# Four banks, an earlier cast and later gathers in the experts of a routed MoE kernel on one core

## Chip, core and metric

The kernel runs on one core of a Trainium2 chip. The metric is the device time of one execution in microseconds.

## What is computed

A linear attention with decay over 4 x 8 heads and 768 steps gives 3072 rows of 384 numbers. They go through a dense mixture block (a * b, then two products, width 1024), and then through eight experts, of which each row is sent to two: the expert's product with w1 (384 x 1024), the positive part, the product with w2 (1024 x 384), weighted and summed into the row. The work around the change is this last part; the shapes below are those of the experts' block.

```python
def _moe2_ref(x, w_gate, w_noise, noise, w1, w2) -> np.ndarray:
    N, D, E, F = (3072, 384, 8, 1024)
...
    for e in range(E):
        for k in range(2):
            mask = top2[:, k] == e
...
            h = np.maximum(x[mask] @ w1[e], 0.0)
            out[mask] += top2_w[mask, k, None] * (h @ w2[e])
    return out.astype(np.float32)

def reference(**kwargs):
...
    attn_out = _attn_ref(**attn_kwargs)
    B, H, S, D = attn_out.shape
    x = np.ascontiguousarray(attn_out.transpose(0, 2, 1, 3)).reshape(B * S, H * D)
    x = _moe_ref(x=x, **moe_kwargs)
    return _moe2_ref(x=x, **moe2_kwargs)
```

## The kernel before

**Numbers in halves.** Every factor is kept as a high part (suffix h) and a low part (suffix l), and a product is three matmuls (mm3, lines 182 to 184: high by high, high by low, low by high). The high part is made by a cast on ScalarE (ACT), the low part by a subtraction on VectorE (DVE).

**The experts.** Expert by expert, 7 row tiles are computed, in two halves: half 0 has the columns of four row tiles (512), half 1 the rest. mm1(hf, ff) is one matmul group of the first layer: nine matmuls into one PSUM bank, for one of eight blocks ff of the hidden width. ACT reads the bank (L889, HH high), then DVE (L890, HH low); then the bank is free. For half 0 the banks are those in MB (two, bA and bB, line 878), taken in turn; for half 1 there are three. mm2(e, j) is the second layer of row tile j: 24 matmuls, then ACT's weighted eviction (L907, ye) and POOL's indirect DMA that adds the rows into the output (L917). The last, small tile has its own form (L912, L914, L916).

**What expert e + 1 needs.** need(e + 1, hf, r): SP loads an index list (L809, ti), POOL gathers the rows (L857, xg). turn(e + 1, hf): SP stores the gathered rows into a buffer in memory (L863) and reads them back transposed (L869, XTx). load_e loads raw weights on SP (L790); split_e casts them (ACT L797, DVE L800). tr(e + 1, hf) casts the transposed rows (XTh: ACT L874, XTl: DVE L875). In second_half (line 931) the row tiles run in the order 0, 6, 1, 2, 3, 4, 5; a quarter of the next weights is cast behind each of the first four, tr(e + 1, 0) stands behind row tile 3 and tr(e + 1, 1) behind row tile 5. first_half(e) issues need and the weight loads for e + 1 and calls turn(e + 1, 0) and turn(e + 1, 1) behind its groups 3 and 6.

**Expert 0** is written out, since its rows come while the router still works: index_first (L817), gather_first (L826), store_first (L831), turn_first (L838); its mm1 groups of half 0 already use four banks, bA, bB, PB[4] and PB[5]. Its first four row tiles of mm2 follow, with need(1, 0, 0) behind the first of them (line 1058), then its second half; behind that turn(1, 0) and the loads of expert 1's first weights, then the remaining row tiles with split_e(1, 0, i).

**What sets the order.** DVE and POOL take their instructions in the order in which the program is written; so do SP's DMAs and those casts of ACT that are pinned with keep_in_program_order. The rest of ACT and PE is ordered by the scheduler. The first weight quarters of expert 0 are cast in the last group of the dense block, in the slots i = 0, 4, 7 and 9 (line 1014).

Of the kernel before, what the change touches and what calls it, by code (L numbers as in the profile page):

```python
# [71 lines left out]
def tile_kernel(ctx: ExitStack, tc: tile.TileContext, dt, nat, w3t, wout, w1, w2, e1, e2, cf, ci, out):  # L72
# [17 lines left out]
    def f(ap):  # L90
        return ap.bitcast(F32)
# [24 lines left out]
    PB = [psum.tile([P, 512], F32, name=f"pb{i}") for i in range(8)]  # L116
    bA, bB, bX, bY, bST, bK = PB[0], PB[1], (PB[2], PB[3]), PB[4], (PB[5], PB[6]), PB[7]
# [674 lines left out]
    def split_e(e, m, i):  # L792
        s = slice(768 * i, 768 * i + 768)
        o = 768 * (i % 2)
        src = RW[e, m, i // 2][:, o:o + 768]
        h, l = (WAh, WBh)[m][:, s], (WAl, WBl)[m][:, s]
        cast = act.copy(out=h, in_=src)  # L797
        if e or m:
            tc.keep_in_program_order(cast)
        dve.tensor_tensor(out=l, in0=src, in1=f(h), op=OP.subtract)  # L800

    def load_idx(e, hf, r):
        TI[e, hf] = EP["a"].tile([P, (TA, TB + 1)[hf], 2], I32, name=f"ti{hf}", bufs=3)
        for o, n, w, j in (((0, TA, TPT, 0),), ((HOLD, TB, TPT, 0), (CAP - TPL, 1, TPL, TB)))[hf]:
            if isinstance(r, int):
                v = table[e * CAPT + r * CAP + o:e * CAPT + r * CAP + o + w * n]
            else:
                v = table[bass.ds(r * CAP + (e * CAPT + o), w * n)]
            tc.keep_in_program_order(sp.dma_start(out=TI[e, hf][:w, j:j + n].rearrange("p j t -> p (j t)"),  # L809
                                                  in_=v.rearrange("(p j) t -> p (j t)", p=w)))  # L810
# [18 lines left out]
    def store_first(j):  # L829
        w = rows_of(j)  # L830
        tc.keep_in_program_order(sp.dma_start(  # L831
            out=rows[0, 2 * TPT * j:2 * TPT * j + 2 * w].rearrange("(p t) d -> p (t d)", t=2), in_=XG[0, j][:w]))

    def turn_first(j, m):

        hf, o = (0, 0) if m <= TPT * TA else (1, 2 * TPT * TA)
        s = slice(2 * TPT * j, 2 * m)
        tc.keep_in_program_order(sp.dma_start_transpose(  # L838
            out=XT["x", hf].bitcast(U16)[:, :, s.start - o:s.stop - o], in_=rows[0, s]))
# [15 lines left out]
    def gather(e, j, rows=NROW):  # L855
        XG[e, j] = EP["b" if e else "a"].tile([P, 2 * DM], U16, name="xg", bufs=NXG)
        pool.indirect_dma_start(out=XG[e, j][:rows_of(j)], out_offset=None, in_=x2d[:rows],  # L857
                                in_offset=bass.IndirectOffsetOnAxis(ap=ti(e, j)[:, 0:1], axis=0))
# [12 lines left out]
    def tr(e, hf):  # L871
        for db in range(3):
            x, h = XT["x", hf][:, db], XT["h", hf][:, db]
            tc.keep_in_program_order(act.copy(out=h, in_=x))  # L874
            dve.tensor_tensor(out=XT["l", hf][:, db], in0=x, in1=f(h), op=OP.subtract)  # L875

    first = True
    MB, MC, AD = (bA, bB), [1], [-1]
    NXG = 7

    def mm1(hf, ff, banks=None):
        n = NAB[hf]
        banks = banks or ((bA, bK, bB) if hf else MB)
        bank = banks[ff % len(banks)][:, :n]
        for kb in range(3):
            w = slice(kb * FF + ff * P, kb * FF + ff * P + P)
            mm3(bank, WAh[:, w], WAl[:, w], XT["h", hf][:, kb], XT["l", hf][:, kb], kb == 0, kb == 2)
        n = (TA, TB)[hf] * TPT
        act.activation(out=Hh[hf][:, ff], in_=bank[:, :n], func=AF.Relu)  # L889
        dve.scalar_tensor_tensor(Hl[hf][:, ff], bank[:, :n], 0.0, f(Hh[hf][:, ff]), op0=OP.max, op1=OP.subtract)  # L890
        if hf == 1:
            dve.tensor_scalar(HM[hf][:, ff], bank[:, n:], 0.0, None, op0=OP.max)

    def mm2(e, j, mid=None):
        hf, jj = divmod(j, TA)
        n, s = rows_of(j), slice(TPT * jj, TPT * jj + rows_of(j))
        MC[0] ^= 1
        bank = bX[MC[0]][:, :DM]
        y = EP["b"].tile([P, DM], F32, name="ye", bufs=9)
        wt = ti(e, j)[:, 1:2].bitcast(F32)  # L900
        if j < NT - 1:
            for ff in range(8):
                if mid and ff == 4:
                    mid()
                w = slice(ff * DM, ff * DM + DM)
                mm3(bank[:n], Hh[hf][:, ff, s], Hl[hf][:, ff, s], WBh[:, w], WBl[:, w], ff == 0, ff == 7)
            act.activation(out=y[:n], in_=bank[:n], func=AF.Copy, scale=wt)  # L907
        else:

            for ff in range(8):  # L910
                g = ff % 4
                pe.matmul(bank[n * g:n * g + n], HM[hf][:, ff], RW[e, 1, ff // 4][:, g * DM:g * DM + DM],  # L912
                          start=ff < 4, stop=ff > 3, tile_position=(0, n * g))
            act.activation(out=y[:n], in_=bank[:n], func=AF.Copy, scale=wt)  # L914
            for g in range(1, 4):
                dve.scalar_tensor_tensor(y[:n], bank[n * g:n * g + n], wt, y[:n], op0=OP.mult, op1=OP.add)  # L916
        ins = pool.indirect_dma_start(out=out, out_offset=bass.IndirectOffsetOnAxis(ap=ti(e, j)[:, 0:1], axis=0),  # L917
                                      in_=y[:n], in_offset=None, compute_op=OP.add).ins

        if j == 0 or AD[0] != e:  # L920
            AD[:] = [e]
        for p in AD[1:]:
            tc.declare_no_dep(ins, p, reason="an expert's rows differ")
        AD.append(ins)

    def need(e, hf, r, rows=NROW):
        load_idx(e, hf, r)
        for j in range(TA) if hf == 0 else range(TA, NT):
            gather(e, j, rows)

    def second_half(e, r, early=True):

        nx = e + 1 < E
        for ff in range(8):
            mm1(1, ff)
            if ff % 2 and early:
                split_e(e, 1, 2 + ff // 4) if ff in (1, 5) else None
        for j in (0, NT - 1, *range(1, NT - 1)):
            mm2(e, j)
            if nx and j < 4:  # L940
                split_e(e + 1, 0, j)
            if nx and j in (3, 5):
                tr(e + 1, j // 5)
        if nx:
            for i in range(2):
                load_e(e + 1, 1, i)
# [37 lines left out]
    for g in range(NGRP):  # L984
        sub = [(mo_ab, g, 0, 0), (mo_ab, g, 0, 1), None, (mo_ab, g, 1, 0), (mo_ab, g, 1, 1), (mo_x, g, 0),
               (mo_ab, g, 2, 0), (mo_ab, g, 2, 1), (mo_x, g, 1), (mo_ab, g, 3, 0), (mo_ab, g, 3, 1), (mo_x, g, 2)]
        if g == 0:
            sub[:5] = [(mo_ab, g, 0, 0, bST[0]), (mo_ab, g, 1, 0, bST[1]), None, (mo_ab, g, 0, 1, bA), (mo_ab, g, 1, 1)]
        if g == NGRP - 1:
            cvx.close()  # L990
            attx.close()
            open_a()
            load_e(0, 0, 0)
            load_e(0, 0, 1)
        for i in range(12):
            if g == NGRP - 1 and i == 7:
                store_first(TA - 1)
                turn_first(TA - 1, TPT * TA)
            if sub[i]:
                act.on = g == 0 and i < 9  # L1000
                fn, *a = sub[i]
                fn(*a)
            elif g:
                mo_x(g - 1, 3)
                mo_lz(g - 1)
                mo_out(g - 1)
            k = SPG * g + i
            run_todo(k - .5, k)
            if i % 3 != 1:
                low_p()  # L1010
            run_todo(k, k + .5)
            act.on = False
            if g == NGRP - 1:
                if i in (0, 4, 7, 9):
                    split_e(0, 0, (0, 4, 7, 9).index(i))
                    if i == 9:
                        load_e(0, 1, 0)
                        load_e(0, 1, 1)
                if i == 0:
                    turn_first(0, TPT * (TA - 1))  # L1020
                if i == 1:
                    index_first(TA - 1, 1)
                    gather_first(TA - 1, NCH - GB)
                if i == 5:
                    tr_first(0, TA - 1)
# [29 lines left out]
    for j in range(TA):  # L1055
        mm2(0, j)
        if j == 0:
            need(1, 0, 0)
            for jj in (NT - 2, NT - 1):
                store_first(jj)  # L1060
            turn_first(NT - 2, CAP)
        if j == TA - 2:
            tr(0, 1)
    need(1, 1, 0)
# [145 lines left out]
```

## Time and profile before

| | us |
|---|---|
| median of 3 runs | 892.7 (891.82 to 895.07) |
| the profiled execution | 900.07 |
| its span in the profile | 898.2 |
| PE busy | 871.3 |
| DVE, ACT, POOL busy | 496.7, 434.3, 243.4 |

Times in the rows are microseconds from the start of the span; the experts' stage begins at about 480 and ends with the span. A row of a timeline tells the start, the duration, the engine, the line of the kernel, the operation, the tile written and the tiles read, and in brackets the idle time of the engine just before it and what ended it. SPq is SP's DMA issue. "PE pb L182 <- DVE HH L890" among the waits is PE's time spent waiting for that step of DVE. Where a row carries "x3", three like instructions are taken together.

### The profile page before, as it was taken

What the parts mean: (1) busy time and instruction counts of PE and PEld (TensorE: products, weight loads), DVE (VectorE), ACT (ScalarE), POOL (GpSimd) and SP (SyncE); (2) the same over time, 40 slices, a digit from 0 to 9 for tenths busy, and PEclk for the clock granted to TensorE, in tenths of its full rate; (3) what the DMA queues carried; (4) which work ended last, traced back from release to release, by engine and by line L of the source; (5) the groups of instructions that cost most, each with busy time, mean ns of one, the idle gap of its engine ahead of it and who ended that gap; (6) DMA issues with size and microseconds to landing.
All of it is one profiled execution on the core that took longest, in us unless ns stands there. A gap on an engine that the chain in (4) does not pass through costs nothing. (4 is left out here: it accounts for less than half of the span.)

```text
span 898.2 us, 18274 instructions
## 1 busy us (share of the span) xinstructions
PE 871.3 (97%) x7333; PEld 807.0 (90%) x7333; DVE 496.7 (55%) x1215; ACT 434.3 (48%) x876; POOL 243.4 (27%) x216
## 2 busy tenths in 40 slices
PE   8999999999999999999999999999999999999994
PEld 5789899999999999999989889898898989999894
DVE  6899866857666667665472553343435335353420
ACT  5777576555556647644452443334334333433420
POOL 2000020141231231232234535216060341603122
PEclk9999999999999999999999999999999999999998
DMA  9955398474575654525145987739185582934113
GB/s 351 391 203 189 95 136 265 117 201 157 133 219 146 190 133 126 147 51 166 36 116 120 266 232 194 187 85 226 50 240 121 145 206 65 228 80 109 18 22 38
DMA packets 123583, 139.22 MB, mean 155 GB/s; under 512 B 74592, under 2 KB 103264, under 8 KB 123488
## 3 DMA queue, kind: packets, MB, share of 16 engines
q1 hardware_dynamic: 99952, 109.58, 42.8%
q0 software_dynamic: 12160, 19.72, 11.4%
q10 hardware_dynamic: 11376, 8.65, 3.0%
q8 instruction: 59, 0.97, 0.5%
q14 instruction: 36, 0.29, 0.1%
HBM read 88.12 MB, written 36.04 MB: 138 GB/s over the span
## 5 line engine op out<-in xcount | busy, mean ns | idle before, releaser
L917 POOL DMA_INDIRECT out<-ye,ti x49 | 77.5, 1582 | 232.5 <-ACT ye L907 212.0
L182 PE MATMUL pb<-XTh,WAh 128*128 128x512 f32 (+1 forms) x384 | 132.5, 346 | 4.8 <-DVE HH L890 3.9
L184 PE MATMUL pb<-XTh,WAl 128*128 128x512 f32 (+1 forms) x384 | 131.3, 342 | 0.0
L183 PE MATMUL pb<-XTl,WAh 128*128 128x512 f32 (+1 forms) x384 | 131.1, 342 | 0.1
L182 PE MATMUL pb<-WBh,HH 128*128 128x384 f32 x384 | 129.3, 337 | 0.0
L184 PE MATMUL pb<-WBh,HH 128*128 128x384 f32 x384 | 128.4, 334 | 0.0
L183 PE MATMUL pb<-WBl,HH 128*128 128x384 f32 x384 | 128.3, 334 | 0.0
L890 DVE SCALAR_TENSOR_TENSOR HH<-pb,HH 128x256 fp32r<-128x256 f32 (+1 forms) x128 | 71.2, 557 | 78.9 <-ACT HH L889 73.2
L889 ACT ACTIVATE HH<-pb 128x256 fp32r<-128x256 f32 (+1 forms) x128 | 62.5, 491 | 106.3 <-PE pb L184 101.5
L907 ACT ACTIVATE ye<-pb,ti 128x384 f32<-128x384 f32 x42 | 24.4, 582 | 139.9 <-PE pb L184 96.0
L733 POOL DMA_INDIRECT slots<-g_sc,g_si x48 | 51.3, 1068 | 134.8 <-DVE g_si L732 69.1
L182 PEld LDWEIGHTS pb<-XTh,WAh 128*128 128x128 f32 x384 | 72.0, 188 | 15.6 <-DVE HH L890 6.5
L182 PE MATMUL pb<-xh,WAh 128*128 128x256 f32 x288 | 81.6, 284 | 0.9 <-ACT WAh L797 0.9
L183 PE MATMUL pb<-xl,WAh 128*128 128x256 f32 x288 | 80.9, 281 | 0.8 <-DVE xl L339 0.8
L183 PE MATMUL pb<-xl,WBh 128*128 128x256 f32 x288 | 81.0, 281 | 0.0
L182 PE MATMUL pb<-xh,WBh 128*128 128x256 f32 x288 | 81.0, 281 | 0.0
L184 PE MATMUL pb<-xh,WBl 128*128 128x256 f32 x288 | 81.0, 281 | 0.0
L184 PE MATMUL pb<-xh,WAl 128*128 128x256 f32 x288 | 80.8, 281 | 0.0
L183 PEld LDWEIGHTS pb<-XTl,WAh 128*128 128x128 f32 x384 | 72.3, 188 | 7.8 <-DVE XTl L875 0.3
L184 PEld LDWEIGHTS pb<-XTh,WAl 128*128 128x128 f32 x384 | 72.2, 188 | 7.7 <-DVE WAl L800 0.2
L182 PEld LDWEIGHTS pb<-WBh,HH 128*128 128x128 f32 x384 | 72.1, 188 | 5.0 <-ACT WAh L797 3.8
L800 DVE TENSOR_TENSOR WAl<-raww,WAh 128x768 fp32r<-128x768 f32 x28 | 26.7, 957 | 87.8 <-ACT WAh L797 70.4
(194 smaller groups left out, 2061.4 us busy)
## 6 DMA issues: line engine op xcount, KB each, us to landing
dtc<-dt SPq DMA_DIRECT2D x24, 772.0 KB
raw<-e SPq DMA_DIRECT2D x18, 768.0 KB
raww<-e SPq DMA_DIRECT2D x14, 768.0 KB
nrk<-nat SPq DMA_DIRECT2D x24, 384.0 KB
expert_rows<-xg SPq DMA_DIRECT2D x45, 192.0 KB
rawf<-w3t SPq DMA_DIRECT2D x16, 512.0 KB
nv<-nat SPq DMA_DIRECT2D x24, 256.0 KB
out<-zeros SPq DMA_DIRECT2D x9, 576.0 KB
```

Of the source, the lines that this page charges most:

```text
L182: pin(pe.matmul(o, wh, xh, start=start, stop=False))
L183: pe.matmul(o, wh, xl, start=False, stop=False)
L184: pe.matmul(o, wl, xh, start=False, stop=stop)
L733: ins = pool.indirect_dma_start(out=table, out_offset=bass.IndirectOffsetOnAxis(ap=si[:, i, k:k + 1], axis=0), in_=SC[:, i, k, :], in_offs ...
L800: dve.tensor_tensor(out=l, in0=src, in1=f(h), op=OP.subtract)
L889: act.activation(out=Hh[hf][:, ff], in_=bank[:, :n], func=AF.Relu)
L890: dve.scalar_tensor_tensor(Hl[hf][:, ff], bank[:, :n], 0.0, f(Hh[hf][:, ff]), op0=OP.max, op1=OP.subtract)
L907: act.activation(out=y[:n], in_=bank[:n], func=AF.Copy, scale=wt)
L917: ins = pool.indirect_dma_start(out=out, out_offset=bass.IndirectOffsetOnAxis(ap=ti(e, j)[:, 0:1], axis=0), in_=y[:n], in_offset=None, com ...
```

## The change

There are four edits. (1) The first layer's half 0 of the experts 1 to 7 uses four banks in place of two. (2) tr(e + 1, 1) stands behind row tile 4 instead of row tile 5. (3) The first quarter of expert 0's w1 is cast in slot 1 of the last group instead of slot 0. (4) need(1, 0, 0), an index load and four gathers, stands behind mm2(0, 1) instead of mm2(0, 0).

```diff
--- before.py
+++ after.py
@@ -875,7 +875,7 @@
             dve.tensor_tensor(out=XT["l", hf][:, db], in0=x, in1=f(h), op=OP.subtract)
 
     first = True
-    MB, MC, AD = (bA, bB), [1], [-1]
+    MB, MC, AD = (bA, PB[4], bB, PB[5]), [1], [-1]
     NXG = 7
 
     def mm1(hf, ff, banks=None):
@@ -939,8 +939,8 @@
             mm2(e, j)
             if nx and j < 4:
                 split_e(e + 1, 0, j)
-            if nx and j in (3, 5):
-                tr(e + 1, j // 5)
+            if nx and j in (3, 4):
+                tr(e + 1, j - 3)
         if nx:
             for i in range(2):
                 load_e(e + 1, 1, i)
@@ -1011,8 +1011,8 @@
             run_todo(k, k + .5)
             act.on = False
             if g == NGRP - 1:
-                if i in (0, 4, 7, 9):
-                    split_e(0, 0, (0, 4, 7, 9).index(i))
+                if i in (1, 4, 7, 9):
+                    split_e(0, 0, (1, 4, 7, 9).index(i))
                     if i == 9:
                         load_e(0, 1, 0)
                         load_e(0, 1, 1)
@@ -1055,10 +1055,11 @@
     for j in range(TA):
         mm2(0, j)
         if j == 0:
-            need(1, 0, 0)
             for jj in (NT - 2, NT - 1):
                 store_first(jj)
             turn_first(NT - 2, CAP)
+        if j == 1:
+            need(1, 0, 0)
         if j == TA - 2:
             tr(0, 1)
     need(1, 1, 0)
```

On ACT, at the boundary between expert 1 and expert 2 (pb_72 to pb_79 are the eight banks; XTh_5968 is the second half of the rows, HH_5971 the first half of the hidden values, ti_6644 the index list of expert 1's second half):

```order
 L907 ACTIVATE ye<-pb_74,ti_6644 128x384
+L874 CAST XTh_5968<-XTx_6509 128x288 x3
 L907 ACTIVATE ye<-pb_75,ti_6644 128x384
-L874 CAST XTh_5968<-XTx_6509 128x288 x3
-L889 ACTIVATE HH_5971<-pb_72 128x512
-L889 ACTIVATE HH_5971<-pb_73 128x512
+L889 ACTIVATE HH_5971<-pb_72 128x512
+L889 ACTIVATE HH_5971<-pb_76 128x512
 L797 CAST WBh<-raw_7274 128x768
```

The three casts moved ahead of the last eviction, and the second group's bank is another one.

On POOL, at expert 0's first row tiles (tf and ti are index lists of expert 0 and expert 1; the four first L857 gather expert 1's half 0, the last three its half 1):

```order
 L826 DMA xg<-x_rows,tf 128x768
 L826 DMA xg<-x_rows,tf 32x768
-L857 DMA xg<-x_rows,ti_6544 128x768 x4
 L917 DMA out<-ye,tf 3968x384
+L857 DMA xg<-x_rows,ti_6574 128x768 x3
+L917 DMA out<-ye,tf 3968x384
+L857 DMA xg<-x_rows,ti_6574 128x768
 L857 DMA xg<-x_rows,ti_6644 128x768 x2
 L857 DMA xg<-x_rows,ti_6644 32x768
```

The gathers of half 0 moved behind the scatter of row tile 0, and the fourth of them behind that of row tile 1.

On SP, at the same place:

```order
 L817 DMA tf<-slots 128x2
 L817 DMA tf<-slots 32x2
-L809 DMA ti_6544<-slots 128x8
-L1107 TENSOR_LOAD rounds
-L1107 ISA x2
+L1108 TENSOR_LOAD rounds
+L1108 ISA x2
 L831 DMA expert_rows<-xg 128x768
 L831 DMA expert_rows<-xg 32x768
 L838 DMA_TRANSPOSE XTx_6509<-expert_rows 128x3x320
+L809 DMA ti_6574<-slots 128x8
 L809 DMA ti_6644<-slots 128x4
```

The index load of expert 1's half 0 moved behind two stores and the transpose of expert 0's last columns. Behind these rows SP's order is the same in both: four stores L863, the transpose L869, two loads L790.

## Rows read from the trace of the kernel before

**Rows 1.** First part of the page: busy time of each engine, share, instructions.

```profile
PE 871.3 (97%) x7333; PEld 807.0 (90%) x7333; DVE 496.7 (55%) x1215; ACT 434.3 (48%) x876; POOL 243.4 (27%) x216
```

**Rows 2.** Waits of PE from 480 to 898 us: total, times, longest.

```profile
PE pb L182 <- DVE HH L890: 3.9, 5, 1.8
```

**Rows 3.** Timeline of PE at the boundaries 1 to 2 and 6 to 7.

```profile
569.58 0.39 PE L184 MATMUL pb<-XTh,WAl 128*128 128x512 f32 x1
570.58 0.50 PE L182 MATMUL pb<-XTh,WAh 128*128 128x512 f32 x1 [0.61 <-DVE HH L890]
570.92 0.39 PE L183 MATMUL pb<-XTl,WAh 128*128 128x512 f32 x1
...
837.30 0.39 PE L184 MATMUL pb<-XTh,WAl 128*128 128x512 f32 x1
837.53 0.39 PE L182 MATMUL pb<-XTh,WAh 128*128 128x512 f32 x1
```

**Rows 4.** Timeline of ACT, then DVE, at the boundary 1 to 2.

```profile
567.67 0.58 ACT L907 ACTIVATE ye<-pb,ti 128x384 f32<-128x384 f32 x1 [3.89 <-remote]
568.15 1.09 ACT L874 CAST XTh<-XTx 128x288 fp32r<-128x288 f32 x3
...
568.61 1.19 DVE L875 TENSOR_TENSOR XTl<-XTx,XTh 128x288 fp32r<-128x288 f32 x3 [6.94 <-ACT XTh L874]
569.83 1.50 DVE L890 SCALAR_TENSOR_TENSOR HH<-pb,HH 128x512 fp32r<-128x512 f32 x2
```

**Rows 5.** Timeline of PE in the last group of the dense block.

```profile
435.00 0.39 PE L182 MATMUL pb<-xh,WAh 128*128 128x256 f32 x1 [0.88 <-ACT WAh L797]
```

**Rows 6.** Timelines of SP, then POOL, then PE, 476 to 500 us.

```profile
476.46 0.81 SPq L817 DMA_DIRECT2D tf<-slots  x2
...
482.26 1.04 SPq L831 DMA_DIRECT2D expert_rows<-xg  x2
485.31 1.27 SPq L838 DMA_TRANSPOSE XTx<-expert_rows  x1
486.62 1.04 SPq L809 DMA_DIRECT2D ti<-slots  x2
487.77 3.46 SPq L863 DMA_DIRECT2D expert_rows<-xg  x4
495.08 3.34 SPq L869 DMA_TRANSPOSE XTx<-expert_rows  x1
498.48 1.10 SPq L790 DMA_DIRECT2D raww<-e  x2
...
479.20 0.98 POOL L826 DMA_INDIRECT xg<-x_rows,tf  x1 [6.35 <-DMA tf<-slots]
...
481.68 0.96 POOL L857 DMA_INDIRECT xg<-x_rows,ti  x1 [0.30 <-issue]
...
485.45 0.95 POOL L857 DMA_INDIRECT xg<-x_rows,ti  x1 [0.30 <-issue]
486.70 1.64 POOL L917 DMA_INDIRECT out<-ye,tf  x1 [0.30 <-issue]
493.10 0.99 POOL L857 DMA_INDIRECT xg<-x_rows,ti  x1 [4.76 <-DMA ti<-slots]
...
491.69 0.40 PE L182 MATMUL pb<-XTh,WAh 128*128 128x288 f32 x1 [0.36 <-ACT XTh L874]
```

**Rows 7.** DMA view, 498.5 to 507 us: queue (packets, MB, share), then an issue.

```profile
q1 hardware_dynamic: 1814, 2.03, 79.5%
...
raww<-e SPq DMA_DIRECT2D x2, 768.0 KB
```

**Rows 8.** Timeline of ACT, then DVE, at expert 1's start.

```profile
507.54 0.82 ACT L797 CAST WAh<-raww 128x768 fp32r<-128x768 f32 x1
...
512.09 1.88 DVE L875 TENSOR_TENSOR XTl<-XTx,XTh 128x512 fp32r<-128x512 f32 x3
```

**Rows 9.** Windows: length; PE, PEld, DVE, ACT, POOL busy; PEclk, DMA share, GB/s.

```profile
886.00:891.20 5.20, 0.04 (x1) 0.00 (x0) 0.00 (x0) 0.58 (x1) 1.56 (x1) 1.00 0.47 65
```

## The prediction

> **What bounds the kernel now.** The page's first part comes first: TensorE (PE) is busy 871.3 of 898.2 us, DVE half of it, ACT and POOL less [rows 1]. So only two things can move the time: a wait of PE that goes or comes. The list of PE's waits over the experts' stage (480 to 898 us) is short; nearly all of it are 3.9 us in five waits for DVE's step L890 [rows 2]. The timeline of PE shows where the first of the five lies, at the boundary between expert 1 and expert 2, at 570.58, and what the same place looks like without it, between experts 6 and 7, where PE goes on at 837.53 [rows 3]. The timelines of ACT and DVE around the first boundary tell the reason [rows 4]. ACT's last eviction of expert 1 (L907) starts at 567.67; behind it in ACT's order stand the three XTh casts of expert 2's second half (568.15); DVE, which runs in program order, takes the XTl steps of these casts at 568.61 and only then, at 569.83, the HH steps (L890) of expert 2's first matmul groups. These groups have two banks in turn, so PE's third group waits until the first bank is read out. Last I read the timelines of SP and POOL where the fourth edit acts (476 to 500 us) and the rows of expert 1's start.
>
> **Four banks and the earlier cast (edits 1 and 2).** They take away the same five waits. In rows 3 the matmul after the wait starts 1.00 us behind its predecessor, where the undisturbed pair has 0.23; and the next starts 0.34 behind it instead of 0.23. A wait listed at 0.61 thus costs 0.77 + 0.11 = 0.88, that is 0.27 more than listed. Five of them: 3.9 + 5 x 0.27 = **5.2 us**. Are all five gone? A group has nine matmuls, 9 x 0.23 = 2.1 us. With four banks the fifth group is the first that needs a bank again, two groups or 4.1 us later than the third; the longest of the five waits is 1.8 [rows 2]. Edit 2 also puts the XTh casts ahead of the last L907, so that the 1.2 us of XTl and the 1.1 us of XTh [rows 4] lie beside PE's last row tile. What is late next is that L907 itself, 1.1 us behind its old place, which only releases a scatter. Either edit would do; both together give 5.2 once, not twice. The bounds are 5.2 and, if ACT's new order only moves the wait, 3.9 - 1.8 = 2.1 (the longest one stays).
>
> The Trainium skill, "TensorE: Matmul & The Clock Gate", section "HAM oscillation — how this bites in real kernels", tells of a kernel in which "Adding PSUM double-buffering gave no further gain". By that the 5.2 would be about 0; the rule fits a PE that waits for DMA, while here the wait ends with DVE's reading of a bank [rows 3], so I go by the row. It would decide in the last rival's favour.
>
> **The weight cast one slot later (edit 3).** On DVE, pp (L589) now stands ahead of WAl (L800); on ACT the cast L797 stays ahead of the eviction L586 there. PE's only wait there is 0.88 at 435.00, and it ends with ACT [rows 5]. ACT's order at this place is the same, so 0; the bounds are 0 and -0.9. The x_rows store and two evictions of ACT behind it change places by under 1 us, with 40 us until the rows are gathered.
>
> **The four gathers later (edit 4).** What goes: the gathers no longer compete with the transposes of expert 0's last columns. PE waits 0.36 for their cast at 491.69 [rows 6]. Nothing says how much of the transpose's time (485.31 to some 491) is contention; the gain is between 0 and 1.0 (the wait, and the slow start behind it), I take 0.5.
>
> What comes: four gathers (L857), their index load (L809), and with them all that SP issues behind. Step by step, all from rows 6:
> 1. The index load stood right behind that of 476.46 in SP's order. Now it stands behind the transpose L838 (485.31 + 1.27), so at 486.6. The two index loads that stood at this very place released POOL at 493.10, after 4.76 us of waiting; the index load of 476.46 released it at 479.20, 2.7 us. So the first gather starts between 489.3 and 493.1 (before: 481.68). The queue carries the transposes then, but the four gathers are gone from it: I take 491.0.
> 2. The fourth starts three pitches of 1.26 later (481.68, then 485.45 for the fourth) and a scatter (1.64 + 0.3; that of row tile 1 now stands between): + 5.7, 496.7. Before: 485.45.
> 3. Gather to the store of its rows: 3.1 at the short end (479.20 to 482.26), 5.4 at the long (485.45 to the end of the four stores' row, 487.77 + 3.46 = 491.2 less one store of 0.3). With few transfers about I take 3.2: 499.9.
> 4. Last store to transpose: 2.5 (the second of the two stores of 482.26, at 482.8, to 485.31) to 4.2 (490.9 to 495.08). I take 4.1, since L869 is the larger transpose: at 504.0 instead of 495.08, **8.9 later** (5.5 by all short ends: 489.3 + 5.7 + 3.1 + 2.5 = 500.6; 13.3 by all long ones: 493.1 + 5.7 + 5.4 + 4.2 = 508.4).
> 5. The loads of expert 1's first weights (L790, 498.48) are issued behind it and move as far. SP's queue moved 2.03 MB in 8.5 us, 239 GB/s [rows 7], so 3.3 us for one of these two 768 KB loads (0.79 MB each): the first lands at 501.8 at the earliest. If the other 0.46 MB of that stretch (stores, the transpose's rest) go ahead of it, it lands (0.46 + 0.79) / 0.239 = 5.2 us after its issue, at 503.7; this I take. It is used at 507.54 by ACT's cast, which waited for nothing then [rows 8]: a slack of 3.8 us (up to 5.7).
> 6. Behind that cast nothing has slack: DVE's XTl steps at 512.09 run without idle time before them, and PE's first group of expert 1, which goes on behind expert 0's last row tile without a gap, needs them [rows 8]. So PE waits 8.9 - 3.8 = **5.1 us** at expert 1's start; from 0 (5.5 - 5.7) to 9.5 (13.3 - 3.8).
>
> The second transfers of expert 1 (turn of its second half, w2 loads) move as well, but are used two groups and more into the expert; by expert 2 SP has caught up.
>
> The Trainium skill, "DMA: Bandwidth & Descriptors", section "Anatomy of one DMA — SWDGE (gpsimd) path", fits a transfer by 2.0 us + bytes / 436 GB/s, an estimate of 3.8 us for 768 KB; the slack would be 5.2, the loss 3.7 and the sum -2.0. The queue's rows show 239 GB/s here, so I keep 3.8 of slack.
>
> **Sum.** -5.2 - 0.5 + 5.1 = -0.6. The profiled execution took 900.07 us (span 898.2), 7.4 above the median of the runs shown; it would come to 899.5. All terms are waits of the experts' stage, so they carry over: 892.7 - 0.6 = **892.1 us**.
>
> **Rivals.**
> - Forecast: the loss at expert 1's start lies between 2.2 and 8: 889.2 to 895.0. Chance 0.64.
> - The delay is hidden: the index load lands in 2.7 us, the gathers' rows are stored at once, and the weights arrive in time (loss 0, at most 1.2). For it: the short ends exist in rows 6. Against: three steps must all be short. 892.7 - 5.7 = 887.0 to 888.2. Chance 0.18.
> - Slower by the late transpose: the gathers queue behind scatters and their landing takes the long end, expert 1 starts up to 9.5 us late, and the wait of 0.36 stays too: 892.7 - 5.2 + 9.5 = 897.0. It decides from a loss of 5.2 on. At its long end PE stands still long enough that the clock matters: in the tail PE did almost nothing from 886.00 to 891.20 and the granted clock was still 1.00 [rows 9]; a stall twice as long has no row here. For it: the two index loads at this place did take the long end. Against: what they competed with is moved away. 895.0 to 897.0, and above if the clock falls: chance 0.11.
> - The edits don't do what they say: the four banks and the cast only move the wait from the third group to a later one. Against: the fifth group comes 4.1 us later. 892.7 - 0.5 + 5.1 = 897.3. Chance 0.07.
>
> **Numbers.** 0.5% of the time, 4.5 us, is about what a measurement of this kernel can tell from no change: faster means below 888.2, slower above 897.2. Faster holds the hidden case and little of the forecast's edge: 0.18. Slower holds half of the last rival and the end of the third: 0.09. The rest, 0.73, is no change: a gain and a loss of the same size. The range, 888.0 to 896.4, leaves out most of the hidden case below and the ends of the last two above.
>
> **What the profile will show.** Right: no wait of PE for L890 at the five boundaries; the gathers L857 of expert 1's first half at about 491; L869 at about 504; a wait of some 5 us of PE at expert 1's first group, ended by ACT's cast of WAh or by DVE; pitches of 52.6 us or so between all experts behind it. Wrong: waits at L890 that remain; an L869 below 501, from which the weights would be in time; a wait that spreads to expert 1's second half because the second turn or the w2 loads come late, which I price at nothing.

## The result: slower, by a wait twice as long as forecast

The changed kernel takes 900.54 us (median of 17 runs) beside 894.47 us for the kernel before (17 runs). The ratio is 1.0064, 95% interval [1.0042, 1.0086]: 0.64% slower. On the 892.7 us that were shown ahead, this is 892.7 x 1.0064 = 898.4 us, above the forecast of 892.1 and above the upper end of the range, 896.4.

Where it went is seen on PE. Its waits from 425 us to the end in the changed kernel, in the columns of [rows 2]:

```profile
PE pb L182 <- ACT XTh L874: 7.6, 1, 7.6
PE pb L183 <- DVE XTl L875: 1.9, 1, 1.9
PE pb L680 <- DVE g_mb L663: 0.6, 1, 0.6
PE pb L182 <- issue: 0.2, 1, 0.2
```

The five waits for L890 are gone, and one long wait has come. To size both, here are the first matmuls of expert 0, 1, 2 and 7 on PE's timeline. Before (512.48 is the last matmul ahead of expert 1):

```profile
457.80 0.39 PE L182 MATMUL pb<-XTh,WAh 128*128 128x512 f32 x1
...
512.48 0.33 PE L184 MATMUL pb<-WBh,HH 128*128 128x384 f32 x1
512.65 0.40 PE L182 MATMUL pb<-XTh,WAh 128*128 128x512 f32 x1
...
565.69 0.39 PE L182 MATMUL pb<-XTh,WAh 128*128 128x512 f32 x1
...
833.41 0.39 PE L182 MATMUL pb<-XTh,WAh 128*128 128x512 f32 x1
```

After:

```profile
456.17 0.39 PE L182 MATMUL pb<-XTh,WAh 128*128 128x512 f32 x1
...
508.85 0.34 PE L184 MATMUL pb<-WBh,HH 128*128 128x384 f32 x1
516.74 0.79 PE L182 MATMUL pb<-XTh,WAh 128*128 128x512 f32 x1 [7.56 <-ACT XTh L874]
519.43 0.79 PE L183 MATMUL pb<-XTl,WAh 128*128 128x512 f32 x1 [1.89 <-DVE XTl L875]
...
573.21 0.39 PE L182 MATMUL pb<-XTh,WAh 128*128 128x512 f32 x1
...
835.57 0.39 PE L182 MATMUL pb<-XTh,WAh 128*128 128x512 f32 x1
```

Four stretches follow from them:

| stretch | before | after | difference |
|---|---|---|---|
| expert 0, first to last matmul | 54.68 | 52.68 | -2.0 |
| from that last matmul to expert 2 | 53.21 | 64.36 | +11.15 |
| expert 2 to expert 7 | 267.72 | 262.36 | -5.4 |
| up to the first matmul of expert 0 | 457.80 | 456.17 | -1.6 |

The last row lies almost wholly ahead of the change and differs from execution to execution. The profiled execution of before was a long one for its kernel (900.07 beside a median of 894.47), so the two executions are only 2.0 us apart; the medians are 6 apart. What the change itself does is the first three rows: -2.0 + 11.15 - 5.4 = +3.8 us in this pair of traces. The other 2 us of the medians have no row here; they would fit a typical execution of before that has less for the edits to win than this long one, which is not shown.

The long wait is a chain on SP, POOL and ACT, whose rows answer to [rows 6]; they begin 2.05 us earlier than there (L838 at 483.26, not 485.31):

```profile
483.26 1.27 SPq L838 DMA_TRANSPOSE XTx<-expert_rows  x1
484.58 1.51 SPq L809 DMA_DIRECT2D ti<-slots  x3
490.64 7.29 SPq L863 DMA_DIRECT2D expert_rows<-xg  x4
500.25 6.64 SPq L869 DMA_TRANSPOSE XTx<-expert_rows  x1
506.95 1.05 SPq L790 DMA_DIRECT2D raww<-e  x2
...
487.33 1.22 POOL L857 DMA_INDIRECT xg<-x_rows,ti  x1 [5.27 <-DMA ti<-slots]
...
493.33 0.98 POOL L857 DMA_INDIRECT xg<-x_rows,ti  x1 [0.30 <-issue]
...
498.31 1.65 POOL L917 DMA_INDIRECT out<-ye,tf  x1 [0.30 <-issue]
500.26 1.58 POOL L917 DMA_INDIRECT out<-ye,tf  x1 [0.30 <-issue]
504.28 1.56 POOL L917 DMA_INDIRECT out<-ye,tf  x1 [2.44 <-ACT ye L907]
...
514.14 0.83 ACT L797 CAST WAh<-raww 128x768 fp32r<-128x768 f32 x1 [10.13 <-DMA raww<-e]
```

Gather, store, transpose, weight load, cast: each is late, and ACT's first cast of expert 1's weights waits 10.13 us for its data. The wait takes the clock with it. The windows of the same stretch (columns as in [rows 9]):

```profile
509.20:516.74 7.54, 0.00 (x0) 0.00 (x0) 1.67 (x3) 2.60 (x5) 0.00 (x0) 0.70 1.06 372
516.74:519.43 2.69, 0.79 (x2) 0.29 (x2) 2.65 (x5) 2.69 (x5) 1.25 (x1) 0.50 1.00 396
519.43:522.90 3.47, 3.47 (x9) 2.79 (x10) 2.89 (x4) 0.23 (x1) 3.47 (x1) 0.56 1.26 163
522.90:530.00 7.10, 7.10 (x33) 5.85 (x32) 3.27 (x5) 3.12 (x5) 5.58 (x6) 1.00 0.91 281
```

PE does nothing for 7.5 us, the granted clock falls to its lower level (0.50, 1.2 GHz), and most of the first matmuls behind the wait run at it (0.56 is the mean over the next nine): nine in 3.47 us, where the undisturbed distance of 0.23 [rows 3] makes 2.1. That is 1.4 us more. The wait itself is (516.74 - 509.02) + (519.43 - 516.97) = 10.2 us, with 509.02 and 516.97 where the two matmuls would have started (0.17 and 0.23 behind the one ahead). Together 11.6, of which the 11.15 above is left, since expert 1 regains some 0.4 us that its third group lost to the two banks before.

### The profile page after: what moved, and what is told of

It is laid out like the page before. It is cut to its first block, busy times and chain, and to the rows that moved or that the text cites. A ratio compares the mean times of both kernels' runs of the same rounds, so it can differ in the third digit from the quotient of the medians.

```text
span 900.3 us, 18273 instructions
## 1 busy us (share of the span) xinstructions
PE 871.3 (97%) x7333; PEld 809.4 (90%) x7333; DVE 495.4 (55%) x1215; ACT 434.8 (48%) x876; POOL 245.8 (27%) x216
## 4 chain that ended last, share of the span: by engine, by line
PE 83%; DVE 7%; DMA 3%; ACT 2%; issue 1%; SPq 1%; POOL 0%; another core or an unknown queue 0%; POOLq 0%; ACTq 0%; DVEq 0%
PE pb L182 25%; PE pb L184 25%; PE pb L183 25%; PE pb L332 3%; PE pb L263 3%; PE pb L912 1%; DMA nrk<-nat 1%; PE pb L296 1%; DVE cvz L166 1%; DMA expert_rows<-xg 1%; DMA rawf<-wout 1%; DMA rawf<-w 1%; DVE w3l L173 1%; DVE fg L210 1%; DVE WAl L800 1%
## 5 line engine op out<-in xcount | busy, mean ns | idle before, releaser
L890 DVE SCALAR_TENSOR_TENSOR HH<-pb,HH 128x256 fp32r<-128x256 f32 (+1 forms) x128 | 71.4, 558 | 108.8 <-ACT HH L889 102.4
L907 ACT ACTIVATE ye<-pb,ti 128x384 f32<-128x384 f32 x42 | 24.5, 582 | 126.2 <-PE pb L184 107.1
```

## The experiments

The theory after the result: the four edits make two effects, a gain of about 5 us at the boundaries (edits 1 and 2) and a loss of about 10 us at expert 1's start (edit 4). The first rival: the edits share in the loss. The runs came in four sets, each on one chip, and the kernel before has another median in each: 898.18 us in the first, 889.01 in the second, 896.40 in the third, 896.58 in the fourth. Ratios are always to the kernel before in the same set. Microseconds against the kernel before are worked out from the ratio; those between two other kernels are differences of medians.

### First set: the edits apart

Everything but the fourth edit (no_gathers_later):

```diff
         if j == 0:
+            need(1, 0, 0)
...
-        if j == 1:
-            need(1, 0, 0)
```

> The changed kernel without its fourth edit: banks, earlier cast and weight cast stay, the index load and the four gathers stand where they stood before. Theory A (the fourth edit alone costs, the others gain as forecast): 5.3 us faster than the kernel before, no wait of PE for L890, equal pitches of 51.05 us between experts, PE enters expert 1 without a wait for weights. Rival B (the four banks or the earlier cast shift transfers of expert 1 and share in the loss): the long wait at expert 1's start stays in part, and the kernel is within 2 us of the one before or slower.

Measured: 892.94 us, ratio 0.9947 [0.9923, 0.9971], 4.8 us faster. There is no wait for L890 and no long wait; PE's only wait behind 480 us is 1.6 us for XTh in expert 0. Theory A holds, but for the distance between experts: from expert 2 on it is an equal 52.47 us, not 51.05.

The fourth edit alone (only_gathers_later):

```diff
         if j == 0:
-            need(1, 0, 0)
...
+        if j == 1:
+            need(1, 0, 0)
```

> The kernel before with the fourth edit alone. Theory A: 9 to 11 us slower than before: PE waits some 9 us at expert 1's start for XTh and XTl, the clock falls to its lower level there, and the five waits for L890 are as before. Rival B (the loss needs the other edits): within 3 us of before.

Measured: 909.92 us, ratio 1.0121 [1.0092, 1.0150], 10.9 us slower. Its waits of PE from 425 us on have both patterns together, the old five and the new long one:

```profile
PE pb L182 <- ACT XTh L874: 5.9, 1, 5.9
PE pb L182 <- DVE HH L890: 4.2, 5, 2.1
PE pb L183 <- DVE XTl L875: 1.9, 1, 1.9
```

The loss is the fourth edit's and needs no other edit. Less the 4.8 us that the other three gain, it makes 6.1 us, beside the 5.7 (0.64%) of all four.

Four banks alone (only_four_banks):

```diff
-    MB, MC, AD = (bA, bB), [1], [-1]
+    MB, MC, AD = (bA, PB[4], bB, PB[5]), [1], [-1]
```

> The kernel before with four banks alone. If either of the two boundary edits is enough, as the prediction says: 5.2 us faster, no wait for L890. Rival (the bank is not what is late, the casts ahead of the HH steps are): 1 to 3 us faster, with waits left at the boundaries.

Measured: 893.42 us, ratio 0.9939 [0.9918, 0.9960], 5.5 us faster, with no wait for L890 left. The banks carry the whole gain. Evictions are still late in this trace, by 1.94, 1.91 and 1.79 us at three boundaries, but PE no longer waits behind them. ACT, then PE, at the boundary between experts 1 and 2:

```profile
565.07 0.58 ACT L907 ACTIVATE ye<-pb,ti 128x384 f32<-128x384 f32 x1 [3.87 <-remote]
...
563.13 0.39 PE L182 MATMUL pb<-XTh,WAh 128*128 128x512 f32 x1
```

The earlier cast alone (only_earlier_cast):

```diff
-            if nx and j in (3, 5):
-                tr(e + 1, j // 5)
+            if nx and j in (3, 4):
+                tr(e + 1, j - 3)
```

> The kernel before with tr(e + 1, 1) behind row tile 4 alone. If either of the two is enough: 5.2 us faster, no wait for L890. Rival (two banks need the HH steps sooner than they come even without the casts ahead): 1 to 3 us faster, with short waits left.

Measured: 896.50 us, ratio 0.9974 [0.9955, 0.9992], 2.3 us faster. The interval excludes 5.2. One wait for L890 is left, at the start of expert 1's second half (1.0 us at 529.19), behind tr(1, 1), which stands in first_half and wasn't moved; the trace of before has no wait there. At the boundary between experts 4 and 5 a rest of 0.35 us stays. So by the medians "either edit would do" holds for the banks alone, and the cast gives under half. At the boundaries themselves it does more: in its trace expert 2 to expert 7 takes 263.12 us, 4.6 less than before. Why the median shows only 2.3 is not shown.

### Second set: a chip without the boundary waits

The third edit alone (only_weight_cast):

```diff
-                if i in (0, 4, 7, 9):
-                    split_e(0, 0, (0, 4, 7, 9).index(i))
+                if i in (1, 4, 7, 9):
+                    split_e(0, 0, (1, 4, 7, 9).index(i))
```

> The kernel before with the third edit alone (first weight quarter of expert 0 cast one slot later). The prediction says 0, with bounds 0 and -0.9 us: the wait of 0.88 near 435 us stays or goes, nothing else changes. Rival (the order it changes on ACT, the x_rows stores behind both evictions, delays the gathers): slower by 1 us or more.

Measured: 888.68 us, ratio 0.9998 [0.9985, 1.0011]: nothing, as forecast. But its trace shows more. This kernel has two banks and the late cast, and yet no wait for L890 anywhere, and equal distances of 52.47 us from expert 2 on. The eviction that was late in [rows 4] (PE's next group at 565.69, L907 at 567.67, 1.98 us behind it) is on time here. ACT and PE at the same boundary:

```profile
561.95 0.58 ACT L907 ACTIVATE ye<-pb,ti 128x384 f32<-128x384 f32 x1 [3.58 <-PE pb L184]
...
561.75 0.39 PE L182 MATMUL pb<-XTh,WAh 128*128 128x512 f32 x1
```

L907 starts 0.20 us behind PE's next group. So the five waits are no fixed property of the kernel; in this execution there was nothing for the banks to win, and none of the four traces of this set has a late eviction at expert 2 or behind. The kernel before is 7 to 9 us faster here than in the other sets.

Where the eviction is late, L907 mostly starts as a scatter of POOL ends. At the boundary of [rows 4], where L907 starts at 567.67, POOL has

```profile
566.05 1.57 POOL L917 DMA_INDIRECT out<-ye,ti  x1 [0.30 <-issue]
```

which ends at 567.62. All traces together hold 21 evictions that are late at a boundary and marked "remote"; 20 of them start within 0.22 us of a scatter's end, while of the evictions not so marked about one in five does. A scatter alone doesn't make an eviction late: in this set they run beside evictions that are on time.

The index load early, gathers later (index_early):

```diff
         if j == 0:
+            load_idx(1, 0, 0)
             for jj in (NT - 2, NT - 1):
...
         if j == 1:
-            need(1, 0, 0)
+            for jj in range(TA):
+                gather(1, jj)
```

> The changed kernel, but the index load of expert 1's half 0 stands where it stood before; only the four gathers come later. Theory A (most of the delay of the gathers is the index load's way round behind the transpose L838; the scatters between the gathers cost little): first gather at about 482.5 instead of 487.3, L869 some 5 us earlier than in the changed kernel, the wait at expert 1's start gone or under 2 us, 4 to 6 us faster than the kernel before. Rival B (the gathers lose by standing behind the scatters): L869 within 2 us of the changed kernel's, and slower than the kernel before.

Measured: 889.05 us, ratio 0.9995 [0.9984, 1.0006], and no wait of PE at all behind 480 us. The loss is gone; L869 went out 8.5 us behind the transpose L838, in the changed kernel 17.0. The 4 to 6 us of gain that theory A had beside it are missing, as this execution has no boundary waits to lose. And the run tells the rivals apart only half: POOL's rows show the four gathers ahead of the first scatter again; the fourth, then the scatter:

```profile
483.76 0.95 POOL L857 DMA_INDIRECT xg<-x_rows,ti  x1 [0.31 <-issue]
485.01 1.64 POOL L917 DMA_INDIRECT out<-ye,tf  x1 [0.30 <-issue]
```

With the index at hand POOL's order puts them back, so POOL does not simply follow the program, as was said ahead of the prediction; it is the index load's place that moves them. The changed kernel's order said so, too: in the program all four gathers stand behind the scatter of row tile 1, in POOL's order three of them stand ahead of it.

The weights first on SP (weights_first):

```diff
-    turn(1, 0)
     load_e(1, 0, 0)
     load_e(1, 0, 1)
+    turn(1, 0)
```

> The changed kernel with the two loads of expert 1's first weights ahead of the stores and the transpose of its rows on SP's queue. Theory A (two things are late, the weights by their place behind the transpose, and the transpose itself, which lands some 12 us after its issue beside POOL's scatters): the casts of the weights are on time, but XTh waits for the transpose; the wait of PE shrinks from 9.5 to about 4 us; 0 to 3 us slower than the kernel before. Rival B (only the weights' place matters): no wait, 5 us faster than before.

Measured: 890.02 us, ratio 1.0005 [0.9992, 1.0019], the same as before. The waits of the changed kernel shrink to 2.7 and 0.2 us, and what PE then waits for is the transpose, as ACT's row tells:

```profile
508.94 1.66 ACT L874 CAST XTh<-XTx 128x512 fp32r<-128x512 f32 x3 [5.02 <-DMA XTx<-expert_rows]
```

Theory A holds in its mechanism: both the weights and the transposed rows are late, and the weights, which set the wait in the changed kernel, by more.

Without two scatters (no_scatters; the sums of expert 0's row tiles 2 and 3 are missing in the output):

```diff
+        if e == 0 and j in (2, 3):
+            return
         ins = pool.indirect_dma_start(out=out, out_offset=bass.IndirectOffsetOnAxis(ap=ti(e, j)[:, 0:1], axis=0),
```

> The changed kernel without the scatter-adds of expert 0's row tiles 2 and 3 (their sums are missing in the output). Theory A (the transpose L869 is slow because those scatters share the DMA engines with it): issue of L869 back to 3.3 us, loads behind it some 4 us earlier, the wait at expert 1's start shrinks by 4 us or more. Rival B (the transpose is slow for another reason, such as the stores just before it): L869's issue stays near 6.6 us and the wait stays above 8 us.

Measured: 895.22 us, ratio 1.0068 [1.0044, 1.0092]. L869's issue takes 3.55 us and the waits are 0.9 and 2.2 us, as theory A has it; but the changed kernel was not on this chip, and the time alone says little. It was repeated in the fourth set.

### Third set: the same kernels on one chip

The kernel before, for its profile (before_again):

> The kernel before itself, for its profile on the same chip as the others of this set. If the chip is one where ACT's last eviction of an expert's row tiles starts 1.8 us or more after PE's next group, the five waits for L890 are there (3.9 us, pitches of about 52 us); if it is one where that eviction starts 0.2 us after it, there are none and all pitches are 51.05 us.

Measured: 895.73 us, ratio 0.9996 [0.9973, 1.0018]. Neither of the two: one wait for L890 of 1.1 us instead of five. A late eviction comes at one boundary and not at the others of the same execution. And the transfers of expert 1 look unlike [rows 6] and [rows 8], though the kernel is the same; SP, POOL and ACT:

```profile
492.25 6.72 SPq L869 DMA_TRANSPOSE XTx<-expert_rows  x1
...
494.59 1.65 POOL L917 DMA_INDIRECT out<-ye,tf  x1 [0.31 <-issue]
...
505.43 0.83 ACT L797 CAST WAh<-raww 128x768 fp32r<-128x768 f32 x1 [0.34 <-DMA raww<-e]
```

L869's issue is twice as long, the first cast of weights has no slack left but waits 0.34 us for them, and PE waits 0.2 us at expert 1's start.

The changed kernel (after_again):

> The changed kernel itself on the same chip. Waits of some 9 us at expert 1's start in either case; 5 to 6 us slower than before where the five waits exist, 10 us or more slower where they don't.

Measured: 902.51 us, ratio 1.0077 [1.0048, 1.0106]; PE waits 7.5 us for XTh and 1.9 for XTl, as expected. It is 6.9 us slower than before, between the two times expected, beside a trace of before with one wait for L890 instead of five or none.

The kernel with the early index load (index_early_2):

> The changed kernel with the index load of expert 1's half 0 where it stood before; with that the gathers, too, go back to their old place in POOL's order, whatever place they have in the program. 5 us faster than before where the five waits exist, the same where they don't.

Measured: 893.65 us, ratio 0.9971 [0.9952, 0.9991], 2.6 us faster than before and 8.9 faster than the changed kernel beside it. Moving one index load back turns the change into a gain. In effect that undoes the fourth edit: in this trace, too, the gathers go ahead of the first scatter.

POOL's order pinned, the gathers behind two scatters (gathers_pinned):

```diff
-        pool.indirect_dma_start(out=XG[e, j][:rows_of(j)], out_offset=None, in_=x2d[:rows],
+        g = pool.indirect_dma_start(out=XG[e, j][:rows_of(j)], out_offset=None, in_=x2d[:rows],
...
+        if e == 1 and j < TA:
+            tc.keep_in_program_order(g)
...
+        if e == 0 and j < 2:
+            tc.keep_in_program_order(sc)
```

> The kernel of the run before, with POOL's order pinned: the four gathers behind the scatters of row tiles 0 and 1, the index load early. The first gather then goes at about 488, as in the changed kernel (487.3). Theory A (the time at which the gathers go is what costs, whether it is the index load or a scatter that holds them): L869 within 2 us of the changed kernel's, a wait of 6 to 9 us at expert 1's start, no gain over before. Rival B (the index load's late landing is the cause, by what it shares the queue with): L869 at least 4 us earlier than the changed kernel's, wait under 3 us.

Measured: 895.63 us, ratio 0.9988 [0.9967, 1.0008], 2 us behind the kernel ahead of it, though the two intervals overlap. The first gather went at 486.12, and the transpose (L871 here) at

```profile
497.26 5.70 SPq L871 DMA_TRANSPOSE XTx<-expert_rows  x1
```

which is 13.4 us behind the transpose L838 (483.83); in the changed kernel of this set it is 17.0 (500.66 - 483.71), in the kernel before 8.4 (492.25 - 483.81). The wait at expert 1's start is 0.4 us. By the numbers named ahead it is between the theories, since the gathers didn't go as late as in the changed kernel: the fourth went at 490.06, there at 493.81. Behind the fourth gather the transpose comes 7.20 us later here and 6.85 there, so it follows the gathers whether the index load or a scatter holds them, which fits theory A's mechanism. Half of the delay comes without the index load's way round and is just swallowed by the slack; no run between this half and the whole was made.

### Fourth set: why 10 us and not 5

The changed kernel (after_third):

> The changed kernel again, beside the next two on the same chip: 9 to 10 us of waiting at expert 1's start, issue of L869 6 to 7 us, first cast of weights 7 us behind the issue of their load.

Measured: 902.49 us, ratio 1.0068 [1.0040, 1.0095]. PE waits 8.7 us, a little under the forecast; issue and cast (6.69 and 6.98 us) are as expected.

Without the two scatters, on the same chip (no_scatters_2):

> The changed kernel without the scatter-adds of expert 0's row tiles 2 and 3 (their sums are missing in the output), on the same chip as the run before. Theory A (the scatters share the DMA engines with the transpose and the loads): weights' cast 5 to 6 us earlier against the transpose L838 than in the run before, wait of PE about 3 us, 5 us faster than the run before. Rival B (chance, or the chip): wait above 8 us and within 2 us of the run before.

Measured: 899.94 us, ratio 1.0038 [1.0020, 1.0056]. This pair can be laid side by side, since L838 stands at 482.95 in one and 482.97 in the other. SP, then ACT, with the scatters (after_third):

```profile
499.88 6.69 SPq L869 DMA_TRANSPOSE XTx<-expert_rows  x1
506.62 1.05 SPq L790 DMA_DIRECT2D raww<-e  x2
...
513.60 0.83 ACT L797 CAST WAh<-raww 128x768 fp32r<-128x768 f32 x1 [9.37 <-DMA raww<-e]
```

and without them (no_scatters_2):

```profile
500.19 3.10 SPq L869 DMA_TRANSPOSE XTx<-expert_rows  x1
503.34 1.05 SPq L790 DMA_DIRECT2D raww<-e  x2
...
508.61 0.83 ACT L797 CAST WAh<-raww 128x768 fp32r<-128x768 f32 x1 [5.42 <-DMA raww<-e]
```

The transpose starts at the same time, but its issue takes 3.10 instead of 6.69 us, the loads follow 3.3 us earlier and the cast 5.0 earlier. PE's waits there are 2.8 + 1.9 = 4.7 us, beside 6.8 + 1.9 = 8.7. In this pair the scatters cost 4.0 us of wait; what stays is about the 5.1 of the forecast. Rival B is out. Theory A holds in its mechanism and is short in size: 4.7 us of wait instead of 3, and the medians differ by 2.6 us, not 5. The traces' 4 flatter it, since the profiled execution without the scatters was the fastest of its ten.

The weights first (weights_first_2):

> The changed kernel with expert 1's first weights loaded ahead of the stores and the transpose of its rows. On the chip of the first trial the wait at expert 1's start fell to 2.7 us. Theory A (the place behind the transpose carries most of the loss): 5 to 7 us faster than the changed kernel on the same chip, 0 to 5 us faster than before, depending on how many of the five waits for L890 the chip shows. Rival B (the transpose is what is late): less than 3 us faster than the changed kernel.

Measured: 898.45 us, ratio 1.0018 [0.9997, 1.0039], 4.0 us faster than the changed kernel beside it, less than the 5 of theory A and more than the 3 of rival B. One wait of 2.8 us for XTh is left, as on the other chip; so both the place of the weights and the transpose share in the loss.

Four banks and the weights first (banks_weights_first), the kernel before with two changes:

> The kernel before with four banks and with expert 1's first weights loaded ahead of the stores and the transpose of its rows; casts, gathers and index load as before. If the weights' place has any price in the kernel before, it is faster than four banks alone (5.5 us faster than before where the five waits exist); I expect 3 to 6 us faster than before where they exist, and the same where they don't, since the weights were in time before.

Measured: 894.50 us, ratio 0.9976 [0.9955, 0.9997], 2.1 us faster than before, under the 3 to 6 expected. No wait for L890 is left, but the loads now run beside the transpose of expert 0's last columns, and PE waits 3.2 us for XTh there. Four banks alone (0.9939) did as well or better, though on another chip. Of the kernels tried, four banks alone is the one to keep; the three edits without the fourth (0.9947, same chip) are as fast.

## Why the prediction was wrong, step by step

- **Boundaries (edits 1 and 2): right in mechanism, and in size for the execution it was read from.** 5.2 us were forecast, 5.4 measured between experts 2 and 7, 5.5 by the banks alone. Wrong was that either edit would do: by the medians the cast alone gives 2.3. And the term was taken as fixed and carried over whole from an execution 7.4 us above the median. It rests on L907 starting 1.98 us behind PE's next group [rows 4], a row that ends with "remote", a releaser the profile doesn't know. In the second set that lateness is absent and the term is worth nothing. Why the eviction is late stays open: PE's matmuls stand in the same places in both traces. Most of the late ones start as a scatter of POOL ends, and between experts 6 and 7, where no transfers for a next expert run, the eviction was on time in every trace; both point to the transfers, but no run here takes them away at the boundaries.
- **PSUM double-buffering** (the Trainium skill, "TensorE: Matmul & The Clock Gate", section "HAM oscillation — how this bites in real kernels"): the page tells of one kernel where it gave no further gain. The first set shows that this doesn't carry over to a wait for a bank's reading: there more banks gave 0.61%.
- **Weight cast (edit 3): right**, nothing.
- **Edit 4, the gain**: 0.5 forecast, 2.0 measured in expert 0 for the pair of traces. It differs by execution: expert 0 takes 52.7 to 53.5 us in the eight traces whose index load stands late, and 52.7 to 54.9 in the eight whose gathers and weight loads stand at their old places.
- **Edit 4, steps 1 to 4: nearly right.** Shifted by the 2.05 us by which this execution is ahead, the forecast has the first gather at 488.95, the fourth at 494.65 and L869 at 501.95. Measured: 487.33, 493.33, 500.25, so 1.3 to 1.7 us earlier than forecast. Part of that is luck, as steps 3 and 4 missed in opposite ways: the last store was issued at 497.60, 4.3 us behind its gather instead of 3.2, and L869 followed 2.65 behind that store instead of 4.1.
- **Edit 4, step 5: the step that failed.** It let the weight loads "move as far" as the transpose. They moved further, since the forecast moved the transpose in time and left its duration, and the time of the loads behind it, as they were: L869's issue took 6.64 us instead of 3.34, and from the loads' issue to the cast it took 7.19 us instead of the 5.2 assumed to the landing. That is 3.3 + 2.0 = 5.3 us that the sum did not hold, less the 1.7 of the steps ahead. In the changed kernel L869 goes out at 500.25, between POOL's scatters of 498.31, 500.26 and 504.28; it took 6.4 to 6.7 us in all four traces with that order, and 3.10 and 3.55 in the two without the first two of these scatters. The fourth set shows the size: without them the wait is 4.7, near the forecast 5.1. But the short issue and the slack that step 5 read are no fixed properties of the kernel before either. In before_again, with the gathers at their old place, the issue was as long as in the changed kernel, and no slack was left at the cast. A further trace of before could have shown both. The prediction named an L869 below 501 as the point from which the weights would be in time; it went out at 500.25 (502.3 with the shift), and they were far from it.
- **The estimate of 3.8 us for a load**: the prediction's own sentence names it as a fit for the gpsimd path, while SP issues these loads [rows 7], so it was no price for them. The first of them held up the cast until 7.19 us behind their issue in the changed kernel and 5.27 without the two scatters, beside the 5.2 assumed.
- **Edit 4, step 6**: the gain in expert 0 brings PE to expert 1's start 2 us sooner, and so takes away as much of the slack of 3.8; this was not counted. From 5.1: + 5.3 - 1.7 + 2.0 gives 10.7, beside the 10.2 measured. The second transfers of expert 1, priced at nothing, cost nothing: no further wait is listed behind the two at its start.
- **The clock**: it fell, as the third rival has it for long waits, and cost 1.4 us. No row of before had shown a price for it.
- **The rivals**: what happened is the third, slower by the late transpose, which was given 0.11 and 897.0 at most, "and above if the clock falls". Its mechanism was told as gathers that land late; what was long was the transpose and the loads. The fourth, that the edits don't do what they say, would give a like time and is refuted by the waits for L890 that are gone.

## What to carry to other kernels

When a transfer is moved, price it anew among its new neighbours: here a transpose between scatter-adds kept neither its issue time nor the start of what was queued behind it. Read such a price and a slack in more than one trace. Look also at what a gain upstream does to the slack downstream, since a consumer that comes earlier makes the same delay longer. And a wait whose releaser the profile can't name should be seen in a second trace before its removal is counted as a gain.

## What was not expected of the hardware

- A DMA transpose's issue on SP is not a constant: the same L869 took 3.34 us [rows 6], 6.64 in the changed kernel, and 3.10 with two scatter-adds left out, on the chip where it took 6.69 with them. With the gathers and loads at their old places it is not constant either. In those eight traces it took 3.2 to 3.4 us where POOL's next scatter starts 1.7 to 1.8 us behind L869, 4.4 where it starts 2.0 behind, and 6.4 to 6.7 where it starts 2.3 behind. What makes the difference was not tried.
- The same kernel before had medians from 889.0 to 898.2 us in different sets, and the difference lies partly in a few late evictions on ACT: five boundaries with 1.8 to 3.2 us in one trace, one in another (2.4 us), none in that of the third edit alone, on the chip with the lowest median.
- In a wait of 7.5 us the granted clock fell to 0.50, and most of the next nine matmuls ran at that level; the window from 522.90 on shows 1.00 again.
